# Ten half chunks of w_in begun later, and two unused tiles that move x, g and w_in, in a fused attention and gated-projection kernel

## The chip, the cores and the metric

The kernel runs on one core of one Trainium2 chip. The metric is the device time of one execution in microseconds; the profile's span runs from the first to the last instruction of the program. In the profile PE is TensorE, with its weight loads apart as PEld; DVE is VectorE, ACT ScalarE, POOL GpSimd and SP SyncE, which issues all DMAs here.

## The reference

An attention with a sigmoid in place of softmax feeds two projections with a gate between them. Inputs are float32.

```python
scores = scale * q @ k.T - log(S)              # B=8, 12 heads, S=448, D=64
x = (sigmoid(scores) @ v)                      # to (B*S, 768) = (3584, 768)
h = x @ w_in                                   # w_in (768, 2048)
g = h * clip(h + 3, 0, 6) / 6
out = g @ w_out                                # w_out (2048, 768)
```

w_in and w_out come as float64; the kernel joins the two 32-bit words of each number by integer operations and arithmetic.

## The kernel before, in words

**Numbers.** The projections and most of the attention multiply in a reduced float32 format (F32R). An operand is therefore split into a high part, rounded, and a low part, the rest; a product takes three matmuls: high by high, high by low, low by high.

**Tiles.** The 3584 tokens lie in seven tiles of 512, t = 0 to 6. The input width 768 makes six blocks of 128, the inner width 2048 makes sixteen chunks fc of 128. `moe_in(t)` is the first projection of one token tile: for each fc 6 x 3 = 18 matmuls (L375) into a PSUM tile ph, 288 for a t. Then ACT (L379) and DVE (L380) turn ph into g, and a DMA puts g into DRAM. ph has two buffers (four in t = 6), so the matmuls of chunk fc wait until L380 of chunk fc - 2 has read its ph. `moe_out` is the second projection (L539): it reads g back, splits it into gh and gl (L499, L500), and multiplies by w_out.

**Three stages.** In the first, heads of the first three batches (18 pairs of heads, 63 score steps) are done in full float32, and meanwhile w_in is brought in. Then `moe_in(0)` runs nearly alone. In the second, the attention of the other five batches and `moe_in` of t = 0 (its last 12 matmuls) to t = 5 are interleaved. In the third `moe_in(6)` runs while w_out is loaded, and then `moe_out`.

**w_in.** It is brought in by 32 half chunks, n = 0 to 31, two for each fc. `load_wi(n)` has three parts: the DMA into a staging tile `st` (L362); `join_f64`, one operation on ACT (L58), five on DVE (L59 to L65) and one on POOL (L68); and `split_f32`, the high part on ACT (L73) and the low part on POOL (L74). From n = 15 on, every n with n % 3 == 2 (17, 20, 23, 26, 29) is staged in a tile called wis, of which there is one buffer; it is also the buffer into which `load` puts q and k of a pair of heads (qkr). The others take wiqh and wiql, two buffers each.

**What sets the order.** Each engine runs its instructions in order. On PE, ACT, DVE and POOL the order is that in which the program is written (`manual_schedule`); SP's DMAs are ordered by the framework's scheduler, and a DMA whose buffer isn't free holds up those behind it. `feed(part, i)` calls part 0, 1 or 2 of half chunk n in step `first[n] + (0, 2, 3)[part]`. Steps 0 to 32 are the loop over the attention, two score steps in each. From step 33 on a step is KU matmuls of `moe_in(0)`: KU = 16 before. At matmul 160 of it (NPL) `load(18)` brings in the pair of heads 18, and at matmul 224 (NPP) `prep(18)` splits it.

**Where the tiles lie.** In the built program, in bytes of a partition: x of even t, in the pool xpr, has its six tiles at 200672 and every 4096 after it, which is 480 past a multiple of 512; x of odd t, in the pool xpl, at 8832 and so on, 128 past. g, in xpr, is 480 past. The tiles of w_in start at 102272 and every 6144 after, 384 past. The operands of the attention are 384 past, with few exceptions. All operands of `moe_out` are 128 past, the last of its g tiles ending at byte 199808.

Of the kernel before, what the change touches and what calls it, by code (L numbers as in the profile page):

```python
# [9 lines left out]
F32 = mybir.dt.float32  # L10
# [8 lines left out]
P = 128  # L19
# [4 lines left out]
NFC = DF // P  # L24
# [10 lines left out]
NSN = PA // 2 * (LN + 1)  # L35
KB = 3
KM = 12
KU = 16
NSL = 4
NWP = 15  # L40
NWA = 22
NPL = 160
NPP = 224
NWU = 1.4
# [62 lines left out]
def tile_kernel(ctx: ExitStack, tc: tile.TileContext, qk, vP, wi, wo, outT):  # L107
# [9 lines left out]

    ph1 = ExitStack()
    ph2 = ExitStack()
    xpr = ph1.enter_context(tc.tile_pool(name="xpr", bufs=1, side="right"))  # L120
    wins = [ExitStack() for _ in range(NG)]
    win = {}
# [5 lines left out]
    ps_s = ph2.enter_context(tc.tile_pool(name="ps_s", bufs=2, space=bass.MemoryType.PSUM))  # L128
    ps_a = ph2.enter_context(tc.tile_pool(name="ps_a", bufs=1, space=bass.MemoryType.PSUM))

    bias_s = xpr.tile([P, 1], F32, name="bias_s")
    nc.gpsimd.memset(bias_s, neg_log_s)
    bias_3 = xpr.tile([P, 1], F32, name="bias_3")
# [208 lines left out]
    def load_wi(n):  # L342

        fc, u = divmod(n, 2)
        hc = NCC // 2
        w = hc * P
        if u == 0:
            wt = win[fc // GF].tile([P, 2, NCC, P], F32R, tag=f"wi{fc}", name=f"wi_{fc}")
            wih[fc], wil[fc] = wt[:, 0], wt[:, 1]
        cs = slice(u * hc, (u + 1) * hc)  # L350
        hi, lo = (w_[fc][:, cs].rearrange("p c f -> p (c f)") for w_ in (wih, wil))
        own = n % NSL if n < NWP else n % (NSL - 1)
        if own == 2:
            sa = att.tile([P, 4 * w], I32, tag="qkr", name=f"wis_{n}", bufs=1)
            st, ab = sa[:, : 2 * w], sa[:, 2 * w :]
        elif own == 3:
            sa = xpl.tile([P, 4 * w], I32, tag="pend", name=f"wis_{n}")
            st, ab = sa[:, : 2 * w], sa[:, 2 * w :]
        else:
            st, ab = (att.tile([P, 2 * w], I32, tag=tag, name=f"wi{tag}_{n}") for tag in ("qh", "ql"))  # L360
        st, ab = st.rearrange("p (n t) -> p n t", t=2), ab.bitcast(F32)
        nc.sync.dma_start(out=st, in_=wi[fc, :, u * w : (u + 1) * w])  # L362
        yield
        join_f64(nc, st, ab[:, :w], ab[:, w:])
        yield
        split_f32(nc, hi, lo, ab[:, :w])
# [18 lines left out]

    NU = (NSN + 1) // 2
    first = [n * NU // NWA for n in range(NWA)]
    first += [NU - 2 + int((n - NWA) * NWU) for n in range(NWA, 2 * NFC)]
    way = {}

    def feed(part, i):
        for n in range(2 * NFC):
            if first[n] + (0, 2, 3)[part] == i:
                if part == 0:
                    way[n] = load_wi(n)
                next(way[n], None)

    with tc.manual_schedule(
# [3 lines left out]
        for i in range(NU + 1):  # L402
            feed(0, i)
            if i == 0:
                load_native(1)
                for u in range(2):
                    for t in blk[u].values():
                        for j in range(2):
                            nc.gpsimd.tensor_copy(t[halves[j], halves[1 - j]], zero[halves[j]])
            feed(1, i)  # L410
            steps = [n for n in (2 * i, 2 * i + 1) if n < NSN]
            for n in steps:
                scores_native(n)
            feed(2, i)
            for n in (2 * i - 2, 2 * i - 1):
                if 0 <= n < NSN:
                    av_native(n)
            for n in steps:
                m, r = divmod(n, LN + 1)
                if r in (0, NC) and (p := 2 * m + 2 + r // NC) < PA:  # L420
                    load_native(p)
        moe = moe_in(0)
        for n in range(NFC * 3 * NCC - KM):
            i, r = divmod(n, KU)
            if r == 0:
# [160 lines left out]
```

## Time and profile before

| | |
|---|---|
| time, median of 3 runs | 1244.57 us (1244.23 to 1244.61) |
| the profiled execution's own time | 1244.73 us |
| its span | 1242.7 us |
| TensorE busy, L375 and L539 | 493.5 us and 3 x 261.4 us |
| TensorE waits before matmuls, L375 and L225 | 13.1 us and 5.5 us |
| mean granted clock of TensorE | 0.995 |

A stretch in the profile is given by its start and end in us from the span's start, with the busy time of each engine in it, the number of its instructions in brackets, and then the clock granted to TensorE (1.00 is full speed) and the share of the DMA engines. In a timeline a row is a run of like instructions of one engine: the start, the time to the end of the last of them, and their count. A matmul overlaps the next one in these rows: it is shown with some 0.39 us, while one starts every 0.23 us, so the spacing of n matmuls is the row's length less 0.39, over n - 1.

### The profile page before, as it was taken

How to read it: one execution, taken by the hardware profiler on the slowest of the kernel's cores; microseconds unless marked ns; L12 is line 12 of the kernel's file. 1: busy time of each engine (PE TensorE's matmuls, PEld its weight loads, DVE VectorE, ACT ScalarE, POOL GpSimd, SP SyncE). 2: the span in 40 equal slices, each digit the busy share in tenths (PEclk: the TensorE clock that was granted, in tenths of full speed). 3: DMA queues.
4: the chain of work that ended last, by engine and by line, in shares of the span. 5: the costliest groups of instructions: out<-in, count | busy, mean ns of one | idle time of the engine just before them, and what ended most of it. 6: DMA issues, size and time to landing. Idle time of an engine off the chain costs nothing.

```text
span 1242.7 us, 15076 instructions
## 1 busy us (share of the span) xinstructions
PE 1220.3 (98%) x5508; PEld 962.1 (77%) x5508; DVE 724.2 (58%) x1284; ACT 519.5 (42%) x671; POOL 256.5 (21%) x297
## 2 busy tenths in 40 slices
PE   8999699999999999999999999999999999999998
PEld 2334487888888888888888888888888888888887
DVE  4566458888888888988888589873030303030300
ACT  6775234666556665665656535322020202020200
POOL 3343343333333433433333000000000000000000
PEclk9999799999999999999999999999999999999999
DMA  7653335334443334433342177734040404040000
GB/s 248 192 169 113 111 114 155 107 93 113 117 111 107 92 113 117 117 110 89 107 117 80 50 220 285 247 105 152 26 161 26 161 26 161 18 161 26 26 26 25
DMA packets 62570, 142.68 MB, mean 115 GB/s; under 512 B 8224, under 2 KB 29728, under 8 KB 58912
## 3 DMA queue, kind: packets, MB, share of 16 engines
q1 hardware_dynamic: 62496, 141.72, 35.9%
q8 instruction: 43, 0.70, 0.2%
q14 instruction: 31, 0.25, 0.1%
HBM read 101.32 MB, written 40.37 MB: 114 GB/s over the span
## 4 chain that ended last, share of the span: by engine, by line
PE 88%; DVE 1%; issue 1%; POOL 0%; ACT 0%; DVEq 0%; POOLq 0%; ACTq 0%
PE po L539 37%; PE ph L375 36%; PE pv L327 6%; PE sc L270 3%; PE sc L271 3%; PE sc L267 1%; PE sc L314 1%; DVE vbh L191 0%; DVE ql L182 0%; DVE g L380 0%; DVE kbl L204 0%; DVE qp L205 0%; DVE al L277 0%; POOL wis L68 0%; POOL wi L74 0%
## 5 line engine op out<-in xcount | busy, mean ns | idle before, releaser
L375 PE MATMUL ph<-x,wi 128*128 128x512 f32 x2016 | 493.5, 395 | 13.1 <-DVE g L380 13.1
L375 PEld LDWEIGHTS ph<-x,wi 128*128 128x128 f32 x2016 | 379.5, 188 | 95.4 <-DVE g L380 14.3
L539 PE MATMUL po<-gl,woh 128*128 128x512 f32 x672 | 261.4, 389 | 0.0
L539 PE MATMUL po<-gh,woh 128*128 128x512 f32 x672 | 261.4, 389 | 0.0
L539 PE MATMUL po<-gh,wol 128*128 128x512 f32 x672 | 261.4, 389 | 0.0
L546 DVE TENSOR_SCALAR o<-po 128x512 f32<-128x512 f32 x42 | 29.0, 689 | 296.5 <-PE po L539 296.5
L499 ACT CAST gh<-gr 128x2048 fp32r<-128x2048 f32 x28 | 53.6, 1914 | 300.6 <-PE po L539 296.4
L277 DVE TENSOR_TENSOR al<-a,ah 128x896 fp32r<-128x896 f32 x120 | 141.1, 1176 | 50.8 <-ACT a L276 49.8
L539 PEld LDWEIGHTS po<-gh,wol 128*128 128x128 f32 x672 | 126.1, 188 | 26.3
L539 PEld LDWEIGHTS po<-gh,woh 128*128 128x128 f32 x672 | 126.1, 188 | 26.2
L539 PEld LDWEIGHTS po<-gl,woh 128*128 128x128 f32 x672 | 126.1, 188 | 26.1
L275 ACT ACTIVATE ah<-sc,bias_s 128x896 fp32r<-128x896 f32 x120 | 109.9, 915 | 74.6 <-PE sc L271 38.5
L178 POOL TENSOR_TENSOR ka<-qkr,ka 64x448 fp32r<-64x448 f32 x60 | 91.9, 1531 | 132.0 <-issue 118.7
L379 ACT ACTIVATE g<-ph,bias 128x512 f32<-128x512 f32 x112 | 77.2, 690 | 93.6 <-PE ph L375 85.0
L276 ACT ACTIVATE a<-sc,bias_s 128x896 f32<-128x896 f32 x120 | 109.2, 910 | 1.6 <-DVE al L277 0.7
L380 DVE SCALAR_TENSOR_TENSOR g<-g,ph 128x512 f32<-128x512 f32 x112 | 76.2, 680 | 31.6 <-ACT g L379 31.2
L500 DVE TENSOR_TENSOR gl<-gr,gh 128x2048 fp32r<-128x2048 f32 x28 | 64.1, 2289 | 29.1 <-ACT gh L499 29.0
L227 ACT ACTIVATE an<-scn,bias_s 128x896 f32<-128x896 f32 x63 | 60.4, 1007 | 23.9 <-PE scn L225 19.1
L270 PE MATMUL sc<-qh,ka 128*128 128x448 f32 x180 | 65.9, 366 | 0.0
L271 PE MATMUL sc<-ql,ka 128*128 128x448 f32 x180 | 65.9, 366 | 0.0
L188 POOL TENSOR_TENSOR vv<-vr,vv 128x192 fp32r<-128x192 f32 x60 | 35.4, 609 | 143.6 <-issue 141.1
L182 DVE TENSOR_TENSOR ql<-qkr,qh 128x896 fp32r<-128x896 f32 x30 | 57.5, 1918 | 5.1 <-ACT qh L181 2.2
(84 smaller groups left out, 1149.2 us busy)
## 6 DMA issues: line engine op xcount, KB each, us to landing
gd<-g SPq DMA_DIRECT2D x112, 256.0 KB, 2.8
gr<-gd SPq DMA_DIRECT2D x28, 1024.0 KB, 5.6
qkr<-qk SPq DMA_DIRECT2D x120, 224.0 KB, 4.0
ws<-wo SPq DMA_DIRECT2D x24, 512.0 KB, 4.8
outT<-o SPq DMA_DIRECT2D x42, 256.0 KB, 2.0
qkn<-qk SPq DMA_DIRECT2D x18, 448.0 KB, 4.3
wiqh<-wi SPq DMA_DIRECT2D x20, 384.0 KB, 3.2
vr<-vP SPq DMA_DIRECT2D x30, 224.0 KB, 2.5
```

Of the source, the lines that this page charges most:

```text
L178: nc.gpsimd.tensor_tensor(out=ka[other, j], in0=kr[other, j], in1=ka.bitcast(F32)[other, j], op=ALU.subtract)
L270: nc.tensor.matmul(sc[:, j, :S], ka[:, j, cs], qh[:, j], start=True, stop=False)
L271: nc.tensor.matmul(sc[:, j, :S], ka[:, j, cs], ql[:, j], start=False, stop=True)
L275: nc.scalar.activation(ah[:, js], sc[:, js, :S], AF.Sigmoid, bias=bias_s, scale=scale)
L276: nc.scalar.activation(a[:, js], sc[:, js, :S], AF.Sigmoid, bias=bias_s, scale=scale)
L277: nc.vector.tensor_tensor(out=al[:, js], in0=a[:, js], in1=ah.bitcast(F32)[:, js], op=ALU.subtract)
L327: nc.tensor.matmul(pv[p][j][:, :S], vv[:, j, c, :], a_[:, j], start=(c == 0 and a_ is ah), stop=(c == NC - 1 and a_ is al),)
L375: nc.tensor.matmul(ph, w[:, cc], x, start=(n == 0), stop=(n == 3 * NCC - 1))
L379: i1 = nc.scalar.activation(g, ph, AF.Relu, bias=bias_3, scale=1.0)
L380: i2 = nc.vector.scalar_tensor_tensor(out=g, in0=g, scalar=6.0, in1=ph, op0=ALU.min, op1=ALU.mult)
L500: nc.vector.tensor_tensor(out=gl, in0=gr, in1=gh.bitcast(F32), op=ALU.subtract)
L539: nc.tensor.matmul(po[t, ec], w[:, fc], x[:, u], start=(fc == 0 and n == 0), stop=(fc == NFC - 1 and n == 2))
```

## The change: other steps for the last ten half chunks, and two tiles that hold nothing

For the half chunks n = 22 to 31 part 0 comes one step later (NU - 1 in place of NU - 2 as the base), and parts 1 and 2 come 3 and 4 steps after it in place of 2 and 3. A step of `moe_in(0)` is 14 matmuls in place of 16. So the split of n = 22 moves from matmul 0 of `moe_in(0)` to matmul 28, and that of n = 31 from matmul 192 to matmul 196. For n below 22 nothing is moved.

A tile of 88 x 4 = 352 bytes at the top end of the memory and one of 104 x 4 = 416 bytes ahead of xpr's first tile are allotted and never used. x of even t now starts at 200320, g at 224896 and w_in at 101504: each 128 past a multiple of 512, as x of odd t and the operands of `moe_out` are. The attention's tiles stay where they were.

```diff
-KU = 16
+KU = 14
...
+    top = ctx.enter_context(tc.tile_pool(name="top", bufs=1, side="right"))
+    top.tile([P, 88], F32, name="top")
     xpr = ph1.enter_context(tc.tile_pool(name="xpr", bufs=1, side="right"))
...
+    xpr.tile([P, 104], F32, name="pad")
     bias_s = xpr.tile([P, 1], F32, name="bias_s")
...
-    first += [NU - 2 + int((n - NWA) * NWU) for n in range(NWA, 2 * NFC)]
+    first += [NU - 1 + int((n - NWA) * NWU) for n in range(NWA, 2 * NFC)]
...
-            if first[n] + (0, 2, 3)[part] == i:
+            if first[n] + ((0, 2, 3) if n < NWA else (0, 3, 4))[part] == i:
```

From L131 on the lines of the changed kernel are numbered 4 higher than before (L379 is L383); `join_f64` and `split_f32` keep theirs.

The order of ACT, from the last score steps of the first stage to the first evacuation of `moe_in(0)`, before. In the names, `wis_23` or `wiql_24` is the staging of that half chunk, `wi_10` the finished chunk 10, `g_0_1` the g of t = 0 and fc = 1; the last number is the tile's own.

```order
L58 ACTIVATE wiql_21_1009<-wiqh_21_1008 128x384
L58 ACTIVATE wiql_22_1013<-wiqh_22_1012 128x384
L73 CAST wi_10_981<-wis_20_982 128x384
L254 CAST x_1_4_774<-pv_16_1003 128x128
L254 CAST x_1_5_779<-pv_17_1029 128x128
L58 ACTIVATE wis_23_1032<-wis_23_1032 128x384
L73 CAST wi_10_981<-wiql_21_1009 128x384
L73 CAST wi_11_1011<-wiql_22_1013 128x384
L58 ACTIVATE wiql_24_1054<-wiqh_24_1053 128x384
L73 CAST wi_11_1011<-wis_23_1032 128x384
L379 ACTIVATE g_0_0_1124<-ph_0_0_1093,bias_3_117 128x512
```

And in the changed kernel:

```order
L58 ACTIVATE wiql_21_1014<-wiqh_21_1013 128x384
L73 CAST wi_10_986<-wis_20_987 128x384
L258 CAST x_1_4_779<-pv_16_1008 128x128
L258 CAST x_1_5_784<-pv_17_1030 128x128
L73 CAST wi_10_986<-wiql_21_1014 128x384
L58 ACTIVATE wiql_22_1035<-wiqh_22_1034 128x384
L383 ACTIVATE g_0_0_1108<-ph_0_0_1082,bias_3_122 128x512
L58 ACTIVATE wis_23_1055<-wis_23_1055 128x384
L73 CAST wi_11_1033<-wiql_22_1035 128x384
L383 ACTIVATE g_0_1_1143<-ph_0_1_1112,bias_3_122 128x512
L58 ACTIVATE wiql_24_1078<-wiqh_24_1077 128x384
L73 CAST wi_11_1033<-wis_23_1055 128x384
```

The evacuation g_0_0 stood behind the work on half chunks 22, 23 and 24; it now stands behind that on 22 alone, and one g comes after each half chunk or two. DVE follows the same pattern: the five operations on half chunk 22, then g_0_0, the five on 23, then g_0_1.

The order of POOL at the same place, before:

```order
L68 TENSOR_TENSOR wis_20_982<-wis_20_982 128x384
L68 TENSOR_TENSOR wiql_21_1009<-wiql_21_1009 128x384
L68 TENSOR_TENSOR wiql_22_1013<-wiql_22_1013 128x384
L74 TENSOR_TENSOR wi_10_981<-wis_20_982,wi_10_981 128x384
L68 TENSOR_TENSOR wis_23_1032<-wis_23_1032 128x384
L74 TENSOR_TENSOR wi_10_981<-wiql_21_1009,wi_10_981 128x384
```

And in the changed kernel:

```order
L68 TENSOR_TENSOR wis_20_987<-wis_20_987 128x384
L68 TENSOR_TENSOR wiql_21_1014<-wiql_21_1014 128x384
L74 TENSOR_TENSOR wi_10_986<-wis_20_987,wi_10_986 128x384
L74 TENSOR_TENSOR wi_10_986<-wiql_21_1014,wi_10_986 128x384
L68 TENSOR_TENSOR wiql_22_1035<-wiql_22_1035 128x384
L68 TENSOR_TENSOR wis_23_1055<-wis_23_1055 128x384
```

L74 of half chunk 20, the last reader of the wis buffer before half chunk 23's DMA, now stands ahead of L68 of half chunk 22 in place of behind it. On TensorE the order is unchanged.

## The prediction

> **What bounds the kernel now.** I read the page's busy table first, then the waits of TensorE, the timeline around the longest of them, and last the busy time by stretch for each token tile.
>
> ```profile
> span 1242.7 us, 15076 instructions
> PE 1220.3 (98%) x5508; PEld 962.1 (77%) x5508; DVE 724.2 (58%) x1284; ACT 519.5 (42%) x671; POOL 256.5 (21%) x297
> PE ph L375 <- DVE g L380: 13.1, 3, 11.7
> ```
>
> TensorE is busy 98% of the span, so time can come from two places only: the little that it waits, and the pace of its matmuls. Of the wait, 13.1 us stand before the first projection (L375), in three pieces, the longest 11.7 us. What removes such a piece shortens the span by it, since TensorE is busy without a break behind it.
>
> The next rows are timelines of one engine each, joined here: start, length, engine, line, what is written and read, and in brackets the idle time ahead and who ended it.
>
> ```profile
> 116.13 8.67 PE L375 MATMUL ph<-x,wi 128*128 128x512 f32 x36
> 136.46 13.76 PE L375 MATMUL ph<-x,wi 128*128 128x512 f32 x50 [11.66 <-DVE g L380]
> ...
> 117.45 0.52 ACT L73 CAST wi<-wis 128x384 fp32r<-128x384 f32 x1 [1.75 <-POOL wis L68]
> 117.87 0.43 ACT L254 CAST x<-pv 128x128 fp32r<-128x128 f32 x2
> 127.67 0.55 ACT L58 ACTIVATE wis<-wis 128x384 f32<-128x384 f32 x1 [9.38 <-DMA wis<-wi]
> 128.12 0.91 ACT L73 CAST wi<-wiql 128x384 fp32r<-128x384 f32 x2
> 132.69 0.55 ACT L58 ACTIVATE wiql<-wiqh 128x384 f32<-128x384 f32 x1 [3.66 <-POOL wi L74]
> 133.55 0.68 ACT L379 ACTIVATE g<-ph,bias 128x512 f32<-128x512 f32 x1
> 135.72 0.68 DVE L380 SCALAR_TENSOR_TENSOR g<-g,ph 128x512 f32<-128x512 f32 x1
> ...
> 105.70 16.86 SPq L362 DMA_DIRECT2D wiqh<-wi  x4
> 124.32 0.33 SPq L362 DMA_DIRECT2D wis<-wi  x1
> 119.35 1.02 POOL L68 TENSOR_TENSOR wiql<-wiql 128x384 f32<-128x384 f32 x1 [1.94 <-DVE wiql L65]
> 122.31 1.01 POOL L68 TENSOR_TENSOR wiql<-wiql 128x384 f32<-128x384 f32 x1 [1.94 <-DVE wiql L65]
> 123.28 1.01 POOL L74 TENSOR_TENSOR wi<-wis,wi 128x384 fp32r<-128x384 f32 x1
> ```
>
> TensorE runs two ph tiles (36 matmuls) and stops: the third needs the buffer of the first, whose evacuation g_0 (ACT L379, then DVE L380) ends at 136.40. ACT is idle from 118.30 to 127.67 for half chunk 23's DMA, with g_0 queued behind it. That DMA was issued only at 124.32, because its one staging buffer was freed by POOL's L74 on half chunk 20 at 124.29; and POOL had first waited for half chunk 22 (L68 at 122.31). Then ACT waits 3.66 us more for half chunk 24's buffer. So the 11.66 us are w_in work standing ahead of g_0 in four in-order queues. From the two TensorE rows, the matmul after the 36th was due at 116.13 + 8.67 - 0.16 = 124.64; it came 11.8 us late.
>
> The wait also costs clock:
>
> ```profile
> 116.00:124.80 8.80, 8.80 (x40) 1.00 0.33 91
> 124.80:136.40 11.60, 0.00 (x0) 0.59 0.12 35
> 136.40:150.00 13.60, 13.54 (x50) 0.85 0.52 164
> ```
>
> These are stretches with TensorE's busy time, then the granted clock: 1.00 ahead of the wait, 0.59 in it, 0.85 behind it. The 50 matmuls from 136.46 take (13.76 - 0.39) / 49 = 273 ns each, against (8.67 - 0.39) / 35 = 237 ns in the 36 before and 233 ns in the steady rows below: 49 x 40 ns = 1.9 us.
>
> The Trainium skill, page "TensorE: Matmul & The Clock Gate", section "Part 1: The HAM clock gate", says that one idle window of about 3.4 us halves the clock. The trace agrees, with 0.59 after 11.66 us; no run here yet shows where the limit lies.
>
> Now the pace. Stretches of the length of one token tile each (t = 1, 2, 3, 4; TensorE's, weight loads', DVE's, ACT's and POOL's busy time, clock, DMA), and under them two 60 us stretches with TensorE alone: t = 6, and the second projection.
>
> ```profile
> 200.60:303.10 102.50, 102.44 (x468) 87.99 (x469) 87.10 (x170) 62.60 (x81) 34.31 (x41) 1.00 0.42 119
> 303.10:407.20 104.10, 104.10 (x469) 87.88 (x469) 87.17 (x168) 63.82 (x83) 37.02 (x42) 1.00 0.38 107
> 407.20:509.60 102.40, 102.40 (x469) 87.90 (x469) 87.06 (x168) 63.84 (x83) 37.62 (x42) 1.00 0.38 109
> 509.60:613.70 104.10, 104.10 (x469) 87.88 (x468) 87.60 (x169) 63.85 (x83) 39.43 (x44) 1.00 0.38 107
> ...
> 720.00:780.00 60.00, 60.00 (x259) 1.00 0.74 251
> 900.00:960.00 60.00, 60.00 (x267) 1.00 0.26 97
> ```
>
> Even and odd tiles do the same 468 or 469 matmuls (288 of L375 each), at full clock and without idle time, yet the even take 1.7 us longer. What differs is where x lies: even t in pool xpr, 480 bytes past a multiple of 512, odd t in xpl, 128 past one. The second projection, whose operands all lie 128 past, runs at 60.39 / 267 = 226 ns a matmul; t = 6, with x at 480 and weights at 384, at 60.39 / 259 = 233 ns (0.39 us is the one matmul that overlaps the edge). I take 6.9 ns a matmul.
>
> **The change part by part.**
>
> *The ten half chunks, later.* No instruction is added or removed. POOL now runs L74 of half chunk 20 ahead of L68 of 22: it follows L68 of 21 (ends 120.37) and ends about 121.4, not 124.29. The DMA of 23 goes then; from issue to ACT took 127.67 - 124.32 = 3.35 us, so it lands about 124.8. On ACT, only L73 of 21 (0.5, from 120.4) and L58 of 22 (0.55) are left ahead of g_0, which ends near 122.1. DVE has the four x and pend copies, then half chunk 22, then g_0:
>
> ```profile
> 119.13 0.35 DVE L59 TENSOR_SCALAR wiql<-wiql 128x384 f32<-128x384 f32 x1
> 119.52 1.07 DVE L60 TENSOR_SCALAR wiql<-wiql 128x384 int32<-128x384 int32 x1
> 121.61 0.56 DVE L65 SCALAR_TENSOR_TENSOR wiql<-wiqh,wiql 128x384 f32<-128x384 uint32 x1
> 128.25 0.36 DVE L59 TENSOR_SCALAR wis<-wis 128x384 f32<-128x384 f32 x1 [4.89 <-ACT wis L58]
> 130.02 0.56 DVE L65 SCALAR_TENSOR_TENSOR wis<-wis 128x384 f32<-128x384 uint32 x1
> ```
>
> Five operations on a half chunk took 3.0 us there (119.13 to 122.17, L60 stretched beside POOL) and 2.3 us here (128.25 to 130.58). From 121.4, with 0.68 for g_0's L380, DVE frees ph_0 between 124.4 and 125.1; TensorE wants it at 124.4: a wait of 0.0 to 0.7 us. For the next one, half chunk 23 reaches DVE at 125.3 and g_1 ends between 128.3 and 129.0; wanted 18 matmuls later, at 129.0. By the same steps g_2 and g_3 stand within 1 us of their times, either side. I take 0.7 us of new wait in all; the bounds are nothing and 3 us (one landing of 3.35 us less the slack). So **13.0 us** are won: 11.8 + 1.9 - 0.7. A wait that short should leave the clock alone: the one of 1.17 us at 200.66 (row below) opens the stretch of t = 1, whose clock is 1.00.
>
> Late next is the end of t = 0. Half chunk 31 is split at matmul 196 instead of 192, and its chunk is wanted at 270: 74 matmuls, 17 us, hide that. Half chunk 29 holds the buffer into which pair 18's q and k go, wanted behind g_11 (matmul 216); before, there was room:
>
> ```profile
> 166.44 0.65 SPq L165 DMA_DIRECT2D qkr<-qk  x1
> 181.17 0.93 ACT L181 CAST qh<-qkr 128x896 fp32r<-128x896 f32 x1
> 194.98 0.94 ACT L181 CAST qh<-qkr 128x896 fp32r<-128x896 f32 x1 [3.27 <-DMA qkr<-qk]
> 200.66 0.73 PE L375 MATMUL ph<-x,wi 128*128 128x512 f32 x2 [1.17 <-DVE g L380]
> ```
>
> 14.7 us lie between the first issue and its use; 29 moves by a few matmuls of 0.23 us, so this cover holds. Pair 19, though, is bound by its load (ACT waits 3.27 us) and sets the 1.17 us wait; that chain starts at g_11 and won't shorten.
>
> *The two unused tiles.* They cost no instruction; x of even t moves from 480 to 128 past a multiple of 512, w_in from 384 to 128. Odd t already have x at 128, so I price an even tile by an odd: 104.1 - 102.4 = 1.7 us each for t = 2 and 4. For t = 6, 288 x 6.9 ns = 2.0 us. For t = 0 only the first 216 matmuls count, 1.5 us, since the last 72 are in the chain just named. Sum **6.9 us**. For w_in's own move I take nothing: odd tiles with weights at 384 do as well as I can price, and the second projection has both at 128. The pace of t = 6 needs room on DVE, which runs the last split of g into gh and gl while TensorE begins the second projection:
>
> ```profile
> 790.23 2.29 DVE L500 TENSOR_TENSOR gl<-gr,gh 128x2048 fp32r<-128x2048 f32 x1
> ```
>
> It ends at 792.5; TensorE, at the second projection from 781.7 on, wants it after 72 matmuls (two output blocks of three groups), 16.3 us later, at 798.0. The 5.5 us between hide the 2.0. Bounds of this part: nothing, and 8.0 us (2.0 for each of four).
>
> The Trainium skill speaks against this part: the same page, section "Back-to-back issue gap", makes the spacing of matmuls a function of the columns alone, N / 2.4 + 2.5 ns, 216 ns for 512. The rows differ from that (226 and 233 ns for the same 512). By this section of the Trainium skill the two tiles win nothing, and the sum would be 13.0 us.
>
> *Sum.* 13.0 + 6.9 = 19.9 us: the span falls from 1242.7 to 1222.8. The profiled execution took 1244.73 us, 2.0 more than its span, so 1224.8; it stands 0.16 above the median, so I forecast **1224.7 us**.
>
> **The rivals.**
>
> *The wait is spread, not gone.* Half chunks 23, 26 and 29 still share one staging buffer, and ACT still meets them ahead of g_1, g_4 and g_7. If each costs 2 us, 6 of the 13.7 us stay: 1244.6 - 7.7 - 6.9 = 1230.0. For it: margins under 1 us above. Against: from 136.46 on the kernel passes 26 and 29 with no wait of TensorE.
>
> *The place modulo 512 is not the cause.* Even tiles may be slow because of the pool, at the far end of the memory, or because of what surrounds them; then 1244.6 - 13.0 = 1231.6 us. Against: t = 6 has no attention around it and is slow, and the second projection is fast with operands up to byte 199808. The Trainium skill's section "Back-to-back issue gap", cited above, would give this time too. A worse form, 128 on both sides colliding, would slow t = 1, 3 and 5 by 1.7 us each: 1236.7; the second projection speaks against it.
>
> *Slower: each of the three wis half chunks stops ACT as 23 does now.* The price is 13.7 us each, 41 us, against 13.7 now: 1244.6 + 27.4 - 6.9 = 1265 us; from one and a half such stops on (20.6 us, what the change wins in all with the old stop) it is slower. For it: same buffer, same queues. Against: POOL's order now frees the buffer before anything that waits.
>
> **How the numbers follow.** Forecast 72%, spread wait 13%, place not the cause 9% (and 2% for collision), slower 4%. The likeliest's own range is 1222 to 1228: nothing to 3 us of new wait, 5 to 8 us for the tiles. With most of the spread wait the range is 1222.0 to 1230.5. A measurement here tells 0.2%, 2.5 us, from no change; all cases but the slower one clear that: faster 95%, same 1%, slower 4%.
>
> **What would show it.** The wait list of TensorE should lose its 11.7 us entry and keep one near 1 us; the clock should stay at 1.00 from 116 to 200 us; ACT should not wait 9 us for wis. The stretches of t = 2, 3 and 4 should be equal, near 102.4 us, and 60 us in t = 6 hold about 267 matmuls. If those stay at 104.1 and 259, the second part is wrong; if g waits of 2 us or more stand at the third to tenth ph tile, the first is.

## The result and the profile after

The changed kernel takes 1224.93 us (1224.56 to 1225.34, 4 runs) against 1244.59 us (1244.23 to 1244.68, 4 runs) of the kernel before in the same runs: a ratio of 0.9843, 95% interval 0.9826 to 0.986. Forecast were 1224.7 us. The profiled execution's span fell from 1242.7 to 1223.2 us.

The page after, and the waits of TensorE:

```profile
span 1223.2 us, 15074 instructions
PE 1212.2 (99%) x5508; PEld 960.8 (79%) x5508; DVE 727.2 (59%) x1284; ACT 519.9 (43%) x671; POOL 256.8 (21%) x297
PEclk9999999999999999999999999999999999999999
PE scn L229 <- DMA qkn<-qk: 4.2, 1, 4.2
PE ph L379 <- DVE g L384: 2.4, 3, 1.3
```

The waits ahead of the first projection fell from 13.1 to 2.4 us, the longest from 11.7 to 1.3 us, and no slice of the span has a reduced clock any more. The timelines of TensorE, ACT, POOL, SP and DVE at the place of the old wait:

```profile
116.01 8.46 PE L379 MATMUL ph<-x,wi 128*128 128x512 f32 x36
125.05 5.32 PE L379 MATMUL ph<-x,wi 128*128 128x512 f32 x22 [0.58 <-DVE g L384]
...
120.28 0.51 ACT L73 CAST wi<-wiql 128x384 fp32r<-128x384 f32 x1 [2.11 <-POOL wiql L68]
120.70 0.54 ACT L58 ACTIVATE wiql<-wiqh 128x384 f32<-128x384 f32 x1
121.15 0.67 ACT L383 ACTIVATE g<-ph,bias 128x512 f32<-128x512 f32 x1
124.38 0.55 ACT L58 ACTIVATE wis<-wis 128x384 f32<-128x384 f32 x1 [2.56 <-DMA wis<-wi]
...
120.20 1.03 POOL L74 TENSOR_TENSOR wi<-wis,wi 128x384 fp32r<-128x384 f32 x1
121.26 0.33 SPq L366 DMA_DIRECT2D wis<-wi  x1
124.32 0.68 DVE L384 SCALAR_TENSOR_TENSOR g<-g,ph 128x512 f32<-128x512 f32 x1
```

POOL frees the staging buffer at 121.23 in place of 124.29, SP issues half chunk 23's DMA at 121.26, and g_0 leaves ACT at 121.82 and DVE at 125.00. ACT still waits for half chunk 23 (2.56 us), but g_0 is ahead of it. TensorE waits 0.58 us for the third ph tile.

The stretches of t = 2, 3 and 4, and 60 us of t = 6 and of the second projection:

```profile
289.20:391.50 102.30, 102.30 (x469) 87.84 (x468) 87.02 (x167) 63.84 (x83) 36.80 (x41) 1.00 0.39 109
391.50:493.90 102.40, 102.40 (x470) 87.91 (x470) 87.24 (x168) 63.88 (x83) 37.81 (x42) 1.00 0.39 109
493.90:596.20 102.30, 102.30 (x469) 87.84 (x468) 87.18 (x168) 63.82 (x83) 39.11 (x43) 1.00 0.39 109
...
700.00:760.00 60.00, 60.00 (x266) 1.00 0.75 254
900.00:960.00 60.00, 60.00 (x267) 1.00 0.17 66
```

Even and odd tiles now take the same time, and t = 6 runs at the second projection's pace.

Where the 19.5 us of the span went, from the first matmul of each t in the two traces: t = 0 (with its end) 13.8 us, t = 2 and t = 4 1.8 us each, t = 6 1.9 us, and about 0.1 us ahead of t = 0. Tiles 1, 3 and 5 are within 0.02 us of before.

### The profile page after: what moved, and what is told of

It reads as the page before. It is cut to its first block, busy times and chain, and to the rows that moved or that the text cites. A ratio compares the mean times of both kernels' runs of the same rounds, so it can differ in the third digit from the quotient of the medians.

```text
span 1223.2 us, 15074 instructions
## 1 busy us (share of the span) xinstructions
PE 1212.2 (99%) x5508; PEld 960.8 (79%) x5508; DVE 727.2 (59%) x1284; ACT 519.9 (43%) x671; POOL 256.8 (21%) x297
## 4 chain that ended last, share of the span: by engine, by line
PE 95%; DVE 2%; ACT 1%; DMA 1%; issue 1%; POOL 0%; SPq 0%; DVEq 0%; POOLq 0%; ACTq 0%
PE po L543 37%; PE ph L379 36%; PE pv L331 6%; PE scn L229 3%; PE sc L274 3%; PE sc L275 3%; PE pv L248 3%; PE sc L318 1%; PE sc L271 1%; ACT an L231 1%; DMA qkn<-qk 1%; PE scn L227 1%; PE pv L246 0%; DMA qkr<-qk 0%; DVE wiql L60 0%
## 5 line engine op out<-in xcount | busy, mean ns | idle before, releaser
L379 PE MATMUL ph<-x,wi 128*128 128x512 f32 x2016 | 485.7, 391 | 2.4 <-DVE g L384 2.4
L379 PEld LDWEIGHTS ph<-x,wi 128*128 128x128 f32 x2016 | 378.0, 188 | 79.0 <-DVE g L384 4.4
L383 ACT ACTIVATE g<-ph,bias 128x512 f32<-128x512 f32 x112 | 77.1, 688 | 69.0 <-PE ph L379 59.9
```

Source lines behind the costliest of these rows:

```text
L379: nc.tensor.matmul(ph, w[:, cc], x, start=(n == 0), stop=(n == 3 * NCC - 1))
L383: i1 = nc.scalar.activation(g, ph, AF.Relu, bias=bias_3, scale=1.0)
```

## The experiments

Where a kernel ran once, spans of the profiled execution are compared. Beside one group of four runs (the two sweeps and the two parts of the steps) the kernel before, run once, had a span of 1245.3 us in place of 1242.7, so a total of that group is no surer than some 3 us, and what the group shows is read from its rows. The second projection, which no edit touches, takes 460.9 us in each of the four traces, as it does before and after the change.

### The steps alone

```diff
-    top = ctx.enter_context(tc.tile_pool(name="top", bufs=1, side="right"))
-    top.tile([P, 88], F32, name="top")
-    xpr.tile([P, 104], F32, name="pad")
```

> The changed kernel without its two unused tiles: x of even t and g are back at 480 past a multiple of 512, w_in at 384. Theory (steps and place are two independent gains, 13.0 and 6.9 us as forecast, 19.7 us measured in all): 1231.6 us, with t = 2 and t = 4 at 104.1 us each and 60 us of t = 6 holding 259 matmuls, and TensorE's longest wait before the first projection near 1 us. Rival (the place modulo 512 is not the cause, the pace came with the steps): near 1224.9 us, with all t at 102.4 us.

Measured: 1231.57 us (4 runs) against 1244.49 (7 runs), ratio 0.9895, interval 0.9879 to 0.9912. That is 12.9 us won. Its stretches of t = 2, 3, 4, and 60 us of t = 6:

```profile
290.50:394.60 104.10, 104.10 (x469) 87.91 (x468) 87.33 (x168) 63.89 (x83) 37.10 (x42) 1.00 0.38 107
394.60:497.00 102.40, 102.40 (x470) 87.89 (x470) 87.02 (x168) 63.85 (x83) 37.72 (x42) 1.00 0.38 109
497.00:601.10 104.10, 104.10 (x469) 87.89 (x468) 87.66 (x169) 63.91 (x83) 39.48 (x44) 1.00 0.38 107
705.00:765.00 60.00, 60.00 (x259) 1.00 0.73 247
```

The even tiles are as slow as before, so the pace did not come with the steps. TensorE's longest wait before the first projection is 1.2 us. The theory holds in its number and in its rows.

### The unused tiles alone

The kernel before, with the three lines above added.

> The kernel before with the two unused tiles alone; the steps of w_in stay as before. Theory: 6.9 us less than before, 1237.7 us; the wait of 11.7 us and the reduced clock behind it stay, t = 2 and 4 take 102.4 us, t = 6 runs at 227 ns a matmul. Rival (place without effect): 1244.6 us. A second rival (the wait absorbs it, since the matmuls ahead of it get faster and only wait longer): about 1238.2, the gain of t = 0 lost in part.

Measured: 1237.52 us (4 runs) against 1244.49, ratio 0.9943, interval 0.9928 to 0.9958: 7.0 us won.

```profile
PE ph L378 <- DVE g L383: 13.6, 3, 11.8
115.89 8.50 PE L378 MATMUL ph<-x,wi 128*128 128x512 f32 x36
136.21 4.11 PE L378 MATMUL ph<-x,wi 128*128 128x512 f32 x9 [11.82 <-DVE g L383]
```

The wait stands, 0.16 us longer, and the matmuls behind it start 427 ns apart (from their starts in the trace, the second to the eighth), against 227 ns further on. From the first matmul of t = 0 to that of t = 1 the unused tiles win 1.3 us of the 1.5 forecast; that the wait absorbs a part, the second rival, thus holds for some 0.2 us, which the total can't tell. The gains of the two parts, 12.9 and 7.0, add up to 19.9 us against 19.7 measured together: they are independent within the scatter of the runs.

### Which tile's place it is: x at 128 with w_in at 384, and x at 480 with w_in at 128

```diff
-    xpr.tile([P, 104], F32, name="pad")
+    xpr.tile([P, 40], F32, name="pad")      # the first: x at 128, w_in at 384
...
-    top.tile([P, 88], F32, name="top")
-    xpr.tile([P, 104], F32, name="pad")
+    xpr.tile([P, 64], F32, name="pad")      # the second: x at 480, w_in at 128
```

> The changed kernel with a smaller second unused tile (160 bytes in place of 416): x of even t and g stay at 128 past a multiple of 512, w_in is back at 384. Theory (x's place alone matters): the same as the changed kernel, 1224.9 us within 0.5, t = 6 at 227 ns a matmul. Rival (w_in's place matters, or x and w_in have to lie alike): even tiles slow again, up to 1231.6 us, or every tile slower by about 1.7 us where they don't lie alike.

> The changed kernel without the first unused tile and with 256 bytes in the second: x of even t and g are at 480 past a multiple of 512, w_in at 128. Theory (x's place alone matters): 1231.6 us, t = 2 and 4 at 104.1 us, t = 6 at 233 ns a matmul. Rival (w_in's place is what helps): 1224.9 us and 227 ns.

Measured: 1225.24 us for the first (span 1223.2, as the changed kernel), 1231.36 us for the second (span 1229.6). 60 us of t = 6 in the one and in the other:

```profile
700.00:760.00 60.00, 60.00 (x266) 1.00 0.75 254
...
704.00:764.00 60.00, 60.00 (x259) 1.00 0.74 250
```

Both agree with the theory that x's place alone matters, and that w_in can lie at 128 or 384. They don't exclude that what matters is how x and w_in lie to each other: 128 and 384 are the same modulo 256, and 480 differs from both by 96 modulo 256.

### A sweep of x's place

```diff
+            if t == 0 and cc:
+                xpr.tile([P, 8], F32, name=f"xp{cc}")
             x = pool.tile([P, 2, T], F32R, tag=f"x{t % 2}{cc}", name=f"x_{t}_{cc}")
...
-    xpr.tile([P, 104], F32, name="pad")
+    xpr.tile([P, 64], F32, name="pad")
```

> The changed kernel with 32 bytes unused ahead of each of x's tiles 1 to 5 of even t, so that the six blocks of x lie at 480, 0, 32, 64, 96 and 128 past a multiple of 512 (w_in stays at 128). Read in t = 6, where the first projection runs alone, by block. Theory (a moving operand is slow where it starts off a multiple of 64 bytes): blocks 0, 2 and 4 at about 233 ns a matmul, blocks 1, 3 and 5 at 227. Rival A (a multiple of 128 is needed): block 3 slow too. Rival B (only a start near the end of 512 is slow): block 0 alone at 233. In time: theory about half of the 6.9 us lost, 1228 us; A 1229; B 1226.

Measured: a span of 1227.5 us, 4.3 above the changed kernel, and no answer by block. The spacings of the matmuls of one chunk of t = 6, taken from their starts in the trace, in ns, three to a block:

```
block 0 (480)  235 235 231
block 1 (  0)  234 229 237
block 2 ( 32)  232 234 238
block 3 ( 64)  229 229 236
block 4 ( 96)  234 231 229
block 5 (128)  234 229 231
```

All blocks are mixed, with a mean of 232.6 ns, block 5 with the good place too. None of the three theories gives that: by each of them block 5 had to run at 227. The total is that of rival A (1229 us is 4.1 above the changed kernel), but the rows are not. Three matmuls are too few for a place to show its pace; the next sweep tells why.

### A sweep of w_in's place

```diff
+            win[fc // GF].tile([P, 8], F32, name=f"wp{fc}")
             wt = win[fc // GF].tile([P, 2, NCC, P], F32R, tag=f"wi{fc}", name=f"wi_{fc}")
...
-    top.tile([P, 88], F32, name="top")
-    xpr.tile([P, 104], F32, name="pad")
+    top.tile([P, 24], F32, name="top")
```

> The changed kernel with 32 bytes unused ahead of each tile of w_in, so that the sixteen chunks lie at sixteen different multiples of 32 past a multiple of 512 (chunk 0 at 320, 1 at 352, ... 5 at 480, 6 at 0, ... 15 at 288), and x of even t at 384. Read by chunk, in t = 6 and in the odd t, whose x is at 128. Theory (the weights' place doesn't matter): every chunk at 227 ns in t = 6 and odd t as before, 1224.9 us. Rival (weights off a multiple of 64 slow the matmul too): odd chunks (1, 3, 5, ...) at 230 ns or more, half of seven tiles, above 1227 us. If x at 384 is slow by itself, all chunks of t = 6 are at 233.

Measured: a span of 1229.7 us, 6.5 above the changed kernel, so the weights' place matters, and the theory that x's place alone does is refuted. The tiles t = 1 to 4 take 103.4 to 103.5 us each, odd ones too. Here a place lasts 18 matmuls. From the starts of the matmuls of t = 6, with x at 384: the mean spacing of the first eight and of the last nine inside a chunk, in ns, by the place of x less that of w_in modulo 256. Each difference occurs in two chunks, 256 bytes apart in place, whose last nine agree within 0.1 ns:

```
x - w_in mod 256   chunks (w_in at)        first 8   last 9
  0                2 (384), 10 (128)        230.6     226.7
 32                1 (352),  9  (96)        233.6     233.3
 64                0 (320),  8  (64)     228.5-230.1  228.9
 96                7  (32), 15 (288)     233.6-233.8  233.3
128                6   (0), 14 (256)        232.4     231.7
160                5 (480), 13 (224)        233.2     233.9
192                4 (448), 12 (192)        233.4     233.6
224                3 (416), 11 (160)        232.5     233.6
```

Neither of the other readings holds: chunks 4 and 12 lie at multiples of 64 and are as slow as the odd chunks, and chunks 2 and 10 run at 226.7 ns with x at 384.

Two things stand here that I had not expected. The pace follows the difference between the places of the moving operand and of the weights, with a period of 256 bytes. And where the difference becomes 0, some seven matmuls pass before the new pace holds (chunks 2 and 10: 236 224 231 236 228 233 231, then 226 and 227); at the other differences the first eight and the last nine lie within 1.2 ns of each other. With w_in at 128 the blocks in the sweep of x stand at differences of 96, 128, 160, 192, 224 and 0: by the table block 5 alone could be fast, and it lasts three matmuls.

### x and w_in alike at another place

```diff
-    top = ctx.enter_context(tc.tile_pool(name="top", bufs=1, side="right"))
-    top.tile([P, 88], F32, name="top")
```

> The changed kernel without the first unused tile: x of even t and g at 480 past a multiple of 512, and w_in at 480 too; x of odd t stays at 128. The sweep of w_in showed that the weights' place matters as well, so two theories stand against each other. Relation (a first projection runs at 227 ns a matmul where x and w_in lie alike modulo 256, wherever that is): t = 6 at 227 ns and t = 2 and 4 at 102.4 us, but the odd tiles, now 128 against 480, slow: t = 1 and 3 at 104.1 us; in all 1224.9 + 3 x 1.7 = 1230.0 us. Absolute (both have to lie 128 past a multiple of 256): t = 6 at 233 ns and every tile at 104.1 us, 1231.6 + 5.1 = 1236.7 us. The theory of the prediction (x alone matters): even tiles slow, odd fast, 1231.6 us.

Measured: a span of 1230.5 us (1233.12 us, one run). 60 us of t = 6, then t = 2 and t = 3:

```profile
707.00:767.00 60.00, 60.00 (x266) 1.00 0.73 252
...
291.40:395.00 103.60, 103.60 (x470) 87.86 (x470) 88.05 (x168) 64.08 (x83) 36.49 (x42) 1.00 0.38 108
395.00:498.60 103.60, 103.60 (x469) 87.91 (x468) 87.31 (x168) 63.76 (x83) 37.88 (x42) 1.00 0.38 108
```

With both at 480, t = 6 runs at the good pace: 480 is no bad place for x, it was bad against weights at 384. The odd tiles, now 128 against 480, are slow, 103.6 us against the 104.1 expected. The relation theory is confirmed by these rows and the other two are refuted. It was wrong for the even tiles of the second stage: 103.6 us, not 102.4, and so its total of 1230.0 us was missed by 3 us. There the first projection alternates with attention matmuls whose operands lie at 384, 96 bytes off modulo 256. The trace shows where the 1.2 us of an even tile lie: 0.86 in its 288 matmuls of the first projection, 0.35 in the 180 of the attention between them. The mean spacing by place in the unbroken runs of 12 matmuls of the first projection in t = 2 (18 such runs in each kernel), in ns; the last is the spacing to the attention matmul behind:

```
x and w_in at 480   234 234 236 224 230 236 229 232 231 227 226 237
changed kernel      231 233 232 229 230 228 227 227 226 227 227 226
```

So the good pace comes here only at the tenth matmul, in the changed kernel at about the seventh. That it is the attention's place which makes the difference is not shown: no run moves it.

### One part of the steps: the later beginning

```diff
-KU = 14
+KU = 16
...
-            if first[n] + ((0, 2, 3) if n < NWA else (0, 3, 4))[part] == i:
+            if first[n] + (0, 2, 3)[part] == i:
```

> The changed kernel with only one of the three changes to the steps: the last ten half chunks begin one step later, but their parts stand 0, 2 and 3 steps after and a step is 16 matmuls, as before. POOL then frees the staging buffer of half chunk 23 early, but ACT and DVE still meet half chunk 23 ahead of the first g. Theory (the queue order decides, and the buffer is freed at 121.2): g of chunk 0 leaves DVE near 128.3 where TensorE wants it at 124.5, a wait of 3.8 us, 1224.9 + 3.2 = 1228.1 us, and 1230 if a wait that long lowers the clock. Rival (it is the buffer alone that made the wait): 1 us of wait, 1225 us. Rival (it needs all three): the old wait, 1238 us.

Measured: a span of 1227.8 us, 4.6 above the changed kernel. The wait, ACT and DVE ahead of it, and the clock:

```profile
128.30 11.88 PE L379 MATMUL ph<-x,wi 128*128 128x512 f32 x44 [3.87 <-DVE g L384]
124.72 0.55 ACT L58 ACTIVATE wis<-wis 128x384 f32<-128x384 f32 x1 [3.96 <-DMA wis<-wi]
125.58 0.68 ACT L383 ACTIVATE g<-ph,bias 128x512 f32<-128x512 f32 x1
127.56 0.68 DVE L384 SCALAR_TENSOR_TENSOR g<-g,ph 128x512 f32<-128x512 f32 x1
125.00:128.00 3.00, 0.00 (x0) 1.00 0.26 100
128.00:140.00 12.00, 11.70 (x44) 0.86 0.51 149
```

As the theory has it: the buffer is freed early, but g_0 behind half chunk 23 costs 3.87 us, 3.3 more than in the changed kernel, and that lowers the clock (0.86 behind it). So the 11.7 us of the old wait come apart: 7.8 us go with the later beginning, of which 2.9 are the earlier buffer (ACT has half chunk 23 at 124.72 in place of 127.67) and the rest half chunk 24, now behind g_0; 3.3 us more go with g_0's place ahead of half chunk 23, which the other two changes give together; 0.6 are left. No run has the later parts (3 and 4 steps after the first) without the shorter step.

### One part of the steps: the shorter step

```diff
-            if first[n] + ((0, 2, 3) if n < NWA else (0, 3, 4))[part] == i:
+            if first[n] + (0, 2, 3)[part] == i:
...
-    first += [NU - 1 + int((n - NWA) * NWU) for n in range(NWA, 2 * NFC)]
+    first += [NU - 2 + int((n - NWA) * NWU) for n in range(NWA, 2 * NFC)]
```

> The changed kernel with only one of the three changes to the steps: a step of the first projection is 14 matmuls in place of 16; the last ten half chunks begin and follow as before. ACT's and POOL's orders up to the first g are then those of before. Theory: the wait of 11.7 us and the lower clock stay, 1237.7 us or a little more, as with the unused tiles alone. Rival (the shorter step is what helps): below 1230 us.

Measured: a span of 1236.4 us, against 1235.6 with the unused tiles alone.

```profile
PE ph L379 <- DVE g L384: 13.8, 3, 11.6
```

The old wait stands. The shorter step by itself wins nothing.

### An attempt at the waits that are left

```diff
-            if first[n] + ((0, 2, 3) if n < NWA else (0, 3, 4))[part] == i:
+            if first[n] + ((0, 2, 3) if n < NWA else (0, 2, 4) if n == NWA else (0, 3, 4))[part] == i:
...
-NPP = 224
+NPP = 204
```

> The first half of that attempt alone: half chunk 22 joined one step earlier. The wait of 0.6 us before the third ph tile goes, the later ones of 0.5 and 1.3 us stay: 1224.3 us, within 0.2% of the changed kernel, so to be read by the waits. If the earlier join puts half chunk 23 behind again, the wait grows to 1 us or more.

> An attempt at a better kernel: the changed kernel with half chunk 22 joined one step earlier (parts 0, 2 and 4 steps after its first; ACT then meets it ahead of the split of 21), and the pair of heads 18 split at matmul 204 in place of 224, so that pair 19's load begins earlier. If the three waits left before the first projection (0.6, 0.5 and 1.3 us) come from those two chains, they go: 1222.6 us. If the load of pair 20, which now stands ahead of a store of g on SP, holds that store up, a wait of 1 to 3 us comes in their place: 1224 to 1227 us.

Measured: the first line alone 1225.6 us (4 runs; ratio to before 0.9847, interval 0.9833 to 0.986), both 1224.8 us (5 runs; 0.9844, 0.9831 to 0.9858). Neither can be told from the changed kernel. The waits of TensorE, its row with the new wait, and ACT and DVE ahead of it, of the second:

```profile
PE ph L379 <- DVE g L384: 2.4, 3, 1.3
137.15 1.20 PE L379 MATMUL ph<-x,wi 128*128 128x512 f32 x4 [0.83 <-DVE g L384]
132.38 0.52 ACT L73 CAST wi<-wiql 128x384 fp32r<-128x384 f32 x1 [2.94 <-POOL wiql L68]
132.80 0.55 ACT L58 ACTIVATE wiql<-wiqh 128x384 f32<-128x384 f32 x1
133.46 1.05 DVE L59 TENSOR_SCALAR wiql<-wiql 128x384 f32<-128x384 f32 x1 [1.67 <-ACT wiql L58]
136.41 0.68 DVE L384 SCALAR_TENSOR_TENSOR g<-g,ph 128x512 f32<-128x512 f32 x1
```

The wait at the third ph tile is gone and another of 0.83 us stands at the sixth, which waits for g_3 (0.86 with the first line alone, where the later waits of 0.5 and 1.2 us stay as expected). DVE does g_3 behind its five operations on half chunk 25, these follow ACT's L58 on it, and that stands behind L73 of half chunk 24, for which ACT waits 2.94 us for POOL. In the changed kernel g_3 ends at 137.54 and the sixth ph tile begins at 137.60: there was no room left. The sum of the three waits is 2.4 us as before: they moved. So neither reading of the two lines came true, though 1224.8 us lies in the range of the second: the new wait comes from w_in's queue, not from a held store.

## Why the prediction was right, and where its reason was not

**The steps: 13.0 us forecast, 12.9 measured.** The order that was read held at each place: POOL's L74 frees the buffer at 121.23 (forecast about 121.4), ACT has half chunk 23 at 124.38 (124.8), g_0 ends on DVE at 125.00 (between 124.4 and 125.1), and TensorE waits 0.58 us (0.0 to 0.7). g_1, g_2 and g_3, forecast within 1 us of their times, caused no wait that the list shows; the matmul behind g_3 starts 0.36 us after the one before it, some 0.1 us late.

**The clock.** Forecast were 1.9 us back from the lower clock; after, no slice of the page shows a reduced clock. With the later beginning alone, 3.87 us of wait lowered the clock and in the changed kernel 1.34 us did not. The Trainium skill, page "TensorE: Matmul & The Clock Gate", section "Part 1: The HAM clock gate", puts the limit at one idle window of about 3.4 us; these two values stand on either side of it. But the time without a matmul does not settle it alone. In the kernel before, the last matmul ended at 124.80, and the clock fell 2.0 us later:

```profile
124.80:126.80 2.00, 0.00 (x0) 1.00 0.61 174
126.90:136.40 9.50, 0.00 (x0) 0.50 0.01 3
```

With the unused tiles alone it fell 2.0 us after the last matmul too, with the shorter step alone 3.4 us, and with the later beginning alone 4.3 us, when matmuls had begun again. So a wait of 2 us may cost clock; the longest before the first projection that did not was 1.7 us (with the shorter step alone).

**The end of t = 0.** It went as forecast in kind and was sized a little low: the waits there grew from 0.25 and 1.17 us to 0.49 and 1.34 us, since the chain from g_11 to pair 19 did not get faster while the matmuls did. The prediction let the last 72 matmuls win nothing, which covers most of this growth. For t = 0 it gives 13.0 + 1.5 = 14.5 us, measured are 13.8; the steps alone won 13.0 there and the tiles alone 1.3.

**The unused tiles: 6.9 us forecast, 7.0 measured alone.** Even tiles win 1.8 us each for 1.7 forecast, t = 6 wins 1.9 for 2.0. Of the 1.8 us only 1.4 lie in the 288 matmuls of the first projection; 0.4 lie in the attention's matmuls between them, which the price, taken from whole tiles, held unseen. But the reason given was wrong in one step: "What differs is where x lies". It is not x's place but the difference between x's and w_in's, modulo 256; with both at 480 the pace is as good as with both at 128. The price held since it came from an odd tile, whose x at 128 and weights at 384 lie alike modulo 256, as 128 and 128 do in the changed kernel; for the same reason "For w_in's own move I take nothing" held. That was luck: w_in moved by 768 bytes, three times 256. Had it been moved by anything but a multiple of 256, that sentence would have failed, as the sweep shows: 228.9 to 233.9 ns in place of 226.7.

**The range.** 1222 to 1228 us does not follow from its terms: the old wait's 13.7 us less 0 to 3 us of new wait, and 5 to 8 us for the tiles, taken from 1244.6 give 1222.9 to 1228.9. The result lies in both.

**The rivals.** The spread wait came in part of the steps only (3.87 us with the later beginning alone). That the place is not the cause is refuted by the steps alone and the tiles alone. That 128 on both sides collides is refuted by t = 6. A stop at each of the three wis half chunks did not come: ACT waits for them (2.56 us for half chunk 23), behind a g. The Trainium skill, page "TensorE: Matmul & The Clock Gate", section "Back-to-back issue gap", gives N / 2.4 + 2.5 ns, a function of the columns alone, for the isolated gap, and for a stream of weight loads and matmuls a sustained 131 ns at 512 columns, which the prediction left out. Neither holds in this kernel: 512 columns took from 226.7 to 233.9 ns with nothing changed but the place of the weights.

## What to carry to other kernels

Where one engine has in-order work of two kinds, look for what stands ahead of the evacuation that frees PSUM: here w_in work for much later chunks held TensorE for 11.7 us, 2.9 of them by a staging buffer that a third engine freed late, the rest by plain order. Two tiles that do the same work at a different pace are a free experiment: price by the faster one, but test which of their differences is the cause before building on it. Where a long run of matmuls is bound by its own pace, let the moving operand and the weights lie alike modulo 256 bytes in a partition; here that was worth 3% of each matmul.

## What was not expected of the hardware

The spacing of matmuls of 512 columns in this reduced float32 format depends on the difference of the two operands' places modulo 256 bytes: 226.7 ns at 0, 228.9 at 64, 231.7 at 128, and 233.3 to 233.9 at the odd multiples of 32 and at 192. Where the difference becomes 0, some seven matmuls pass before 226.7 ns hold, and between attention matmuls up to nine, so short runs do not reach the good pace. What in the chip makes it so, no run here shows.
